# A written-out order of every queue in place of a greedy scheduler: clustered attention and a gated long convolution on one core

## The chip, the core and the metric

The kernel runs on one core of one Trainium2 chip. Five engines work from queues of their own: PE (TensorE, matrix products into PSUM), DVE (VectorE), ACT (ScalarE), POOL (GpSimd) and SP (SyncE, which here only issues transfers). The metric is device microseconds of one execution. Several executions are timed, and their median is the time of the kernel; one more is profiled.

## The reference

Two parts, cut to what matters. The first is attention in which a query sees only the keys of its own cluster (batch 4, 8 heads, 768 positions, 64 values a head, 16 centroids a head):

```python
q_assign = np.argmax(np.einsum('bhsd,hcd->bhsc', q_n, c_n), axis=-1)
k_assign = np.argmax(np.einsum('bhsd,hcd->bhsc', k_n, c_n), axis=-1)
mask = q_assign[:, :, :, None] == k_assign[:, :, None, :]
scores = scale * np.matmul(q, k.transpose(0, 1, 3, 2))
scores = np.where(mask, scores, -1000000000.0)
scores = scores - np.max(scores, axis=-1, keepdims=True)
attn = np.exp(scores)
attn = attn / (np.sum(attn, axis=-1, keepdims=True) + 1e-09)
return np.matmul(attn, v).astype(np.float32)
```

The second takes its output, as (4, 768, 512), through a gated convolution over the whole sequence:

```python
proj = x @ w_proj
x1, x2, x3 = (proj[..., :D], proj[..., D:2 * D], proj[..., 2 * D:])
X2 = np.fft.rfft(x2, n=S, axis=1)
H = np.fft.rfft(filter_fft, n=S, axis=0)[None, :, :]
x2_conv = np.fft.irfft(X2 * H, n=S, axis=1)
y = x1 * x2_conv * x3
return (y @ w_out).astype(np.float32)
```

## The kernel before

**Work.** `build` describes the whole computation as a list of 1917 operations, made in the order of the mathematics. An operation (`Plan.op`) holds a function that emits its instructions, the engines that may run it with an estimated duration on each, what it reads and writes, and, where it writes PSUM, a `Bank` that it allocates and later operations free. PSUM has eight banks; banks 4 and 5 together hold the attention output (`pair`) for most of the run.

**Stages.** Attention runs in 8 groups `n` (a batch element and half of its heads), each of 2 pairs of heads `pr`, so 16 blocks. Before a group, `routing(n)` transposes its queries and keys on PE (L564, L575), evicts them into `qkP` (L265 on ACT or L267 on DVE), casts them into the bf16 tiles `aug` (the same lines; ACT, DVE or POOL), multiplies with the centroids (L484, L595), finds the nearest centroid on DVE (L616 to L633) and puts the one-hot rows into `aug` by transfers (L469), so that one product gives the masked scores. A block (`attention`) has 6 steps of 128 keys. A step is 3 score operations on PE (`sc`, through the helper `product`, L73 and L75), 3 exponentials on ACT into `p` (L678, L681) and one value product of 8 matmuls into `pair` (L692). The row sums are built on DVE by adding the `p` tiles into `acc` (L713); the first sum of a block is split into three parts that DVE or POOL can run (`part`, L709). Then ACT copies the output to `osb` (L716), the denominators come from a matmul (`den`, L726) or, in the middle groups, from transfers that add rows (L746), their reciprocal (L759) is spread over the partitions by transfers (L760, L763), and DVE writes the normalised output `xT` (L792).

After every second group `hyena(b)` runs the convolution of one batch element, between the products of the next attention blocks: projections (L824), spectra (L75, L458), products with the filter's spectrum on DVE (L848), their sums `y` on DVE or POOL (L852), gates `x3` (L885, L888), inverse transforms (L75), evictions `od` and `sd` (L911, L913), folds on DVE or POOL (`fold`, L923), the gated result `y2` (L926) and the output product, evicted into `ob` (L946) and stored (L953). `tables` makes the transform tables and the filter's spectrum `hm` (L441 to L445) at the start, `weights` loads `w_proj` in four pieces (`wpj`, L1020) and `w_out` (L1023) from POOL's queue. `load_qk` (L302) and `load_v` (L308) load queries, keys and values from SP's queue, the first ones also from ACT's.

**Who sets the order.** Every instruction order is fixed when the program is built. `Plan.place` simulates the five engines with the estimated durations: each time it takes the engine that can start earliest, and for it, among the operations that could start within `wait` of the earliest one, the one with the smallest due time. The due time of an operation is written at its `op(...)` call and shifted by its entry in the table `NUDGE` (some 1900 numbers). Further terms are costs: a change of PE's array mode (`shape`), two value products in a row (`bonus`), an operation on DVE that another engine could run (`BUSY`). `ONLY` pins an operation to one engine. `banks_for` picks the PSUM banks: those that come free first, at most `HELD` banks each for the scores and for the rest. The result is one list sorted by planned start; the program is emitted in that order, so the list is each engine's queue. An engine never overtakes: an operation that waits holds all behind it on the same engine.

**PE's array mode.** `array` gives each PE operation a mode: 128 columns, 64 or 32. A score or projection takes the mode of the operation ahead of it, if that was 64 or 128; in 64 `product` emits it as two halves.

**POOL and DVE.** An operation with `lock` on POOL waits for the last `lock` operation that stands before it on DVE (the last lines of the kernel's function, at the end of the file).

Of the kernel before, what the change touches and what calls it, by code (L numbers as in the profile page):

```python
# [35 lines left out]
LEAD = 2.99901  # L36
FIRST = 2
BUSY = 8.09741
HELD = 4
# [38 lines left out]
class Plan:  # L78

    def __init__(self):
        self.ops, self.writers, self.reads = [], {}, {}

    def op(self, eng, fn, due, r=(), w=(), alloc=None, free=(), lock=False, byts=0, after=(), kind=None, lat=0.0):
        o = Op()
        o.eng = eng if isinstance(eng, dict) else {eng[0]: eng[1]}
        o.fn, o.due, o.alloc, o.free, o.lock, o.byts, o.kind = fn, due, alloc, free, lock, byts, kind
        o.seq = len(self.ops)
        o.due += NUDGE.get(o.seq, 0.0)  # L90
        o.outs, o.end, o.start, o.on = [], None, None, None
# [15 lines left out]
        for d in deps:  # L107
            d.outs.append(o)
        for h in free:
            h.readers += 1  # L110
        self.ops.append(o)
        return o

    def place(self, free0, banks_for, switch=0.1, wait=0.1, rate=215e3, bonus=10.84378, margin=0.02195, shape=1.63806):
        free = dict(free0)
        bank_free = [0.0] * 8
        ready = {e: [] for e in free}
        pend = 0
        st = SimpleNamespace(pool=0.0, dve=0.0, bw={}, last=None, kind=None, score=0, o=0, tail=0,
                             held=dict(score=0, fill=0, o=0))  # L120
# [3 lines left out]
        def enqueue(o):  # L124
# [4 lines left out]
            for e in o.eng:  # L129
                ready[e].append(o)  # L130
# [1068 lines left out]
```

## Time and profile before

| | before |
|---|---|
| time, median of 3 runs | 386.62 us (385.18 to 389.62) |
| span of the profiled execution | 383.4 us |
| PE busy | 366.2 us, 96% |
| DVE busy | 335.8 us, 88% |
| ACT busy | 258.7 us, 67% |
| POOL busy | 115.3 us, 30% |
| TensorE clock granted, mean | 0.997 |
| moved by DMA | 47.19 MB |

The span runs from the first to the last instruction of the profiled execution; its own run time outside that span is not given, so the time of the runs, 3.2 us longer at the median, stands beside it. Busy times are unions over an engine's instructions. In the rows of groups the parts are: line, engine, operation, tile written and tiles read, shapes, count, busy us, mean ns of one, and the idle time of the engine just before them with what ended it. Line numbers are those of the kernel before. A matmul's end is modelled in the profile, and matmuls in different columns of the array overlap, so eight value matmuls of 490 ns mean take 1.30 us together.

### The profile page before, as it was taken

The numbers are of one execution on the slowest core, as the hardware profiler recorded it, in microseconds if no ns is written. First come the engines' busy times: TensorE is split into PE (matmuls) and PEld (weight loads), VectorE is DVE, ScalarE is ACT, GpSimd is POOL, SyncE is SP. The second block draws the span as 40 slices with busy tenths as digits, with TensorE's granted clock in tenths as the row PEclk, the third lists the DMA queues.
The fourth block names the chain that finished last, engine by engine and source line by source line (L and its number), as shares of the span: only waits on it lengthen the run. The fifth ranks groups of instructions, "written<-read, shape, count | busy, mean of one in ns | idle before, by whom it ended". The sixth has DMA issues, their size and how long they took to land.

```text
span 383.4 us, 8667 instructions
## 1 busy us (share of the span) xinstructions
PE 366.2 (96%) x3337; PEld 223.0 (58%) x3343; DVE 335.8 (88%) x497; ACT 258.7 (67%) x483; POOL 115.3 (30%) x155
## 2 busy tenths in 40 slices
PE   3999997999999999999999999999999899999995
PEld 2555454445455564655465665667578566557883
DVE  8778797888899689988999997998998899999982
ACT  5998878787885986588784656877762458712142
POOL 8522302011014454322342443222330452212500
PEclk9999999999999999999999999999999999999998
DMA  9909967642688678466986888854666641200124
GB/s 174 237 21 208 192 151 153 149 96 78 138 164 163 111 145 143 97 114 105 194 132 163 124 166 212 131 77 77 105 97 162 146 68 9 78 11 2 55 113 164
DMA packets 93861, 47.19 MB, mean 123 GB/s; under 512 B 82088, under 2 KB 87676, under 8 KB 93820
## 3 DMA queue, kind: packets, MB, share of 16 engines
q1 hardware_dynamic: 87836, 36.84, 43.3%
q0 software_dynamic: 2704, 8.98, 16.3%
q10 hardware_dynamic: 3280, 0.82, 1.2%
q8 instruction: 26, 0.43, 0.5%
q14 instruction: 15, 0.12, 0.1%
HBM read 31.59 MB, written 7.40 MB: 102 GB/s over the span
## 4 chain that ended last, share of the span: by engine, by line
PE 73%; DVE 17%; ACT 4%; issue 3%; POOL 1%; DVEq 0%; POOLq 0%; ACTq 0%
PE bank L75 30%; PE pair L692 24%; DVE acc L713 8%; PE bank L824 6%; PE bank L564 3%; PE bank L73 2%; PE bank L595 2%; PE bank L458 2%; DVE hm L445 1%; ACT p L681 1%; PE bank L726 1%; PE bank L608 1%; PE bank L575 1%; ACT qkP L265 1%; DVE mx L616 1%
## 5 line engine op out<-in xcount | busy, mean ns | idle before, releaser
L692 PE MATMUL pair<-p,vraw 128*64 128x385 f32 x768 | 143.1, 490 | 0.3 <-ACT osb L716 0.2
L681 ACT ACTIVATE p<-bank 128x512 f32<-128x512 f32 x192 | 110.1, 609 | 26.3 <-PE bank L75 20.1
L713 DVE TENSOR_TENSOR acc<-p,acc 128x1536 f32<-128x1536 f32 x64 | 112.9, 1763 | 10.6 <-POOL acc L709 4.4
L692 PEld LDWEIGHTS pair<-p,vraw 128*64 128x64 f32 x768 | 56.1, 136 | 46.2 <-issue 39.0
L75 PE MATMUL bank<-aug,aug 128*64 128x256 bf16 (+3 forms) x652 | 70.2, 326 | 1.4 <-DVE tm L267 1.3
L678 ACT ACTIVATE p<-bank 128x512 f32<-128x512 f32 x96 | 58.0, 608 | 12.3 <-PE bank L75 12.1
L75 PEld LDWEIGHTS <-aug 80*64 80x64 bf16 (+1 forms) x652 | 40.0, 109 | 33.5 <-issue 23.0
L746 POOL DMA_DIRECT2D acc<-acc x30 | 24.2, 807 | 65.6 <-DVE acc L713 26.0
L75 PE MATMUL bank<-xT,wpj 128*64 128x384 bf16 x448 | 41.5, 326 | 0.0
L709 POOL TENSOR_TENSOR acc<-p,p 128x512 f32<-128x512 f32 x22 | 28.1, 1282 | 44.0 <-DVE acc L709 21.1
L267 POOL CAST aug<-qkP 64x768 bf16<-64x768 f32 x22 | 18.0, 821 | 68.9 <-DVE acc L713 25.7
L75 PEld LDWEIGHTS <-y 128*64 128x64 bf16 x512 | 29.8, 110 | 9.8 <-issue 4.8
L265 ACT COPY qkP<-bank 128x512 f32<-128x512 f32 (+1 forms) x47 | 23.7, 542 | 17.4 <-PE bank L75 9.4
L75 PEld LDWEIGHTS <-wpj 128*64 128x64 bf16 x448 | 28.0, 110 | 11.9 <-issue 3.8
L848 DVE TENSOR_TENSOR tm<-bank,hm 128x512 f32<-128x512 f32 x44 | 28.5, 683 | 4.8 <-POOL y L852 1.6
L852 POOL TENSOR_TENSOR y<-tm 128x512 bf16<-128x512 f32 x17 | 21.5, 1273 | 23.3 <-DVE acc L713 9.6
L265 ACT CAST aug<-qkP 64x768 bf16<-64x768 f32 x31 | 25.7, 829 | 1.7 <-DVE qkP L267 0.5
L75 PE MATMUL bank<-wout,y 128*64 128x512 bf16 x192 | 23.1, 379 | 0.0
L824 PE MATMUL bank<-wpj,xT 128*64 128x512 bf16 x192 | 22.6, 380 | 0.0
L709 DVE TENSOR_TENSOR acc<-p,p 128x512 f32<-128x512 f32 x26 | 17.7, 700 | 2.5 <-ACT p L681 1.8
L716 ACT COPY osb<-pair 128x770 f32<-128x770 f32 x16 | 12.9, 804 | 9.8 <-PE pair L692 9.6
L923 POOL TENSOR_TENSOR yy<-sd 128x384 f32<-128x384 f32 x9 | 9.0, 1003 | 33.4 <-DVE acc L713 15.1
(154 smaller groups left out, 456.9 us busy)
## 6 DMA issues: line engine op xcount, KB each, us to landing
vraw<-in_v_dram SPq DMA_DIRECT2D x16, 384.0 KB, 4.5
qkraw<-in_q_dram SPq DMA_DIRECT2D x30, 192.0 KB, 4.7
qkraw<-in_k_dram SPq DMA_DIRECT2D x30, 192.0 KB, 5.2
rb<-dr SPq DMA_DIRECT2D x30, 192.0 KB, 3.5
out_dram<-ob SPq DMA_DIRECT2D x11, 512.0 KB, 3.1
acc<-acc POOLq DMA_DIRECT2D x10, 384.0 KB, 5.6
acc<-acc POOLq DMA_DIRECT2D x10, 192.0 KB, 4.0
y<-in_moe_filter_fft_dram SPq DMA_DIRECT2D x4, 384.0 KB, 5.2
```

The costliest lines, as they stand in the source:

```text
L75: T.nc.tensor.matmul(out[64 * i:64 * i + 64], lhsT[:, 64 * i:64 * i + 64], rhs, start=start, stop=stop)
L265: T.nc.scalar.copy(out, in_)
L267: (T.nc.vector if e == "DVE" else T.nc.gpsimd).tensor_copy(out, in_)
L678: T.nc.scalar.activation(o, ap(h).rearrange("p (a b) -> p a b", a=2), Act.Exp, scale=0.125)
L681: T.nc.scalar.activation(flat(s)[:, lo:lo + 512], ap(h), Act.Exp, scale=0.125)
L692: T.nc.tensor.matmul(o[64 * hp:64 * hp + 64, ch, :385], T.vraw[vs][:, hp, sk * D:(sk + 1) * D], T.p[slots[sk]][:, hp, 384 * ch:384 * ch + ...
L709: alu(e).tensor_tensor(o, x, y, op=Alu.add)
L713: T.nc.vector.tensor_tensor(T.acc[os], T.p[slots[sk]][:, :, :S], T.acc[os], op=Alu.add)
L746: op(("POOL", .8), lambda e, rows=rows: T.nc.gpsimd.dma_start(flat_()[:rows], flat_()[rows:2 * rows], accum_op=Alu.add), te, r=[], w=AK, b ...
L824: T.nc.tensor.matmul(ap(h)[64 * i:64 * i + 64], T.xT[xs][:, kt, c:c + 64], T.wpj[:, kt, DM:2 * DM], start=kt == 0, stop=kt == ND - 1)
L848: op(("DVE", .68), lambda e, i=i, cs=cs, r=r, h=h: T.nc.vector.tensor_tensor(T.tm[r][:, cs], ap(h), hmrow(i, (0, 2, 2, 3)[2 * r + cs]), op ...
L852: op({"POOL": 1.5, "DVE": .68}, lambda e, i=i, r=r: alu(e).tensor_tensor(T.y[:, i, r], T.tm[r][:, 0], T.tm[r][:, 1], op=Alu.add if r else ...
```

## The change

`Plan.place` and `banks_for` go, with the due-time shifts `NUDGE`, the pins `ONLY` and the scheduler's constants. In their place stands a string `ORDER` with one word for each operation: a letter for the engine, the number of the operation in the list of `build`, and after a colon the PSUM banks where it allocates some. `Plan.follow` reads the words, sets engine and banks, and returns the operations in the order of the words; PE's array mode follows from that order by the same `array` as before. The operations themselves, their functions, what they read and write, and the emission are untouched. The due times in `build` stay in the file and are no longer read.

```diff
 ROWS = 16
-LEAD = 2.99901
 FIRST = 2
-BUSY = 8.09741
-HELD = 4
 EARLY = 8.73655
-NUDGE = {0:-2.65714,1:-0.164318,2:15.6428,3:104.959,
...
-ONLY = {23:"SP",24:"SP",25:"SP",26:"ACT",27:"ACT",29:"SP",30:"ACT",53:"ACT",
...
+ENGINE = {"P": "PE", "A": "ACT", "V": "DVE", "G": "POOL", "S": "SP"}
 THIRDS = [[(0, 0, 512)], [(0, 512, 768), (1, 0, 256)], [(1, 256, 768)]]
-HOLD = {"score": "score", "o": "o"}
-AFTER = {"PE": .16}
-OVERLAP = {"ACT": .09, "DVE": .08}
...
-        o.due += NUDGE.get(o.seq, 0.0)
...
-    def place(self, free0, banks_for, switch=0.1, wait=0.1, rate=215e3, bonus=10.84378, margin=0.02195, shape=1.63806):
...
-        return sorted(self.ops, key=lambda o: (o.start, o.seq))
...
-def banks_for(bank, free, st, o):
...
+    def follow(self, order):
+
+        placed, last = [], None
+        for word in order.split():
+            name, _, banks = word.partition(":")
+            o = self.ops[int(name[1:])]
+            o.on = ENGINE[name[0]]
+            if banks:
+                o.alloc.ids = tuple(map(int, banks))
+            if o.on == "PE":
+                last = array(o, last)
+                o.whole = last == 128
+            placed.append(o)
+        assert len({o.seq for o in placed}) == len(placed) == len(self.ops)
+        return placed
+
+
+ORDER = """
+G8 A15 S24 A23 G13 S26 A25 G1 S27 G10 V4 S28 V16 V17 G0 V18 V43 A19 S29 G7 V6 V31 S108 V37 G2 V20 P54:0 G5 P52:1 G9
...
+P349:1 P355:3 V323 G353 P357:2 A350 P359:6 S324 P363:7
...
+V1897 P1899 A1900 S1901
+"""
...
-    order = P.place({"PE": .3, "ACT": .8, "DVE": .8, "POOL": .8, "SP": .8}, banks_for)
+    order = P.follow(ORDER)
     return P, order
```

Counted over both built programs, 129 operations change their engine (the rest of the difference is place and bank). By line, the number on each engine before and after:

| operation | ACT | DVE | POOL |
|---|---|---|---|
| casts into `aug` (operation at L581) | 31, 23 | 11, 12 | 22, 29 |
| first sums `part` (L701) | | 26, 28 | 22, 20 |
| products `y` (L852) | | 7, 16 | 17, 8 |
| folds (L917) | | 23, 29 | 9, 3 |
| gated result `y2` (L926) | | 15, 14 | 1, 2 |
| evictions into `qkP` (L567, L577) | 40, 42 | 12, 10 | |
| evictions `x3`, `od` (L885, L911) | 37, 41 | 11, 7 | |
| tables `inv`, scaling (L407, L411, L439) | 11, 10 | 4, 5 | |

More of the change, by code (lines that the diff above doesn't have):

```diff
@@ L223, in banks_for @@
-def banks_for(bank, free, st, o):
-    def whole(lo, hi):
-        return max(free[lo:hi])
-    if bank.cls == "o":
-        t = whole(4, 6)
-        return ((4, 5), t) if t < 1e8 else None
-    allowed, first = [0, 1, 2, 3, 6, 7], []
-    if st.score and st.score < st.scores:
-        if st.held["score" if bank.cls == "score" else "fill"] + bank.n > HELD:
-            return None
-    if st.o == 0:
-        allowed += [4, 5] if bank.cls == "head" else []
-    elif st.o == st.otiles:
-        if st.tail:
-            allowed += [4, 5]
-        elif whole(4, 6) < 1e8:
-            first += [4, 5]
-    t = lambda i: whole(4, 6) if i in first else free[i]
-    ids = sorted((i for i in allowed + first if free[i] < 1e8), key=lambda i: (t(i), i))[:bank.n]
-    return (tuple(ids), max(map(t, ids))) if len(ids) == bank.n else None
+    def follow(self, order):
[12 more added lines that the diff above has]
+        return placed
@@ new lines @@
+G669 P767:1 P747 S712 V519 S711 V520 S710 V756 P521:0 S709 P769:7 P755 A770 A768 V522 P848:637 V524 V523 V764 P526:1
+A850 S886 P763 A849 A766 A851 V772 P529:0 P786:2 P788:3 P790:6 A787 P793:7 V527 P771 A791 G774 A789 V525 S670 V530
+S887 G855 P537:2 A773 V528 P795:6 S713 P797:3 G853 A794 P792:45 V531 A796 V533 A798 P803:1 V854 S671 P805:7 P807:0
+V532 P534:6 A806 S715 A808 S847 P811:3 G801 P813:7 V536 P799 S885 A814 V535 A804 S888 V538 G775 A812 P856:076 V539
+A852 V800 P815:1 P542:3 A858 V859 A857 V540 P544:2 A816 V541 P819:0 A543 P821:6 P546:7 V802 V672 P823:1 P827:3 A547
@@ new lines @@
+P809 A824 V673 V545 S674 A820 G776 V810 A822 P829:7 P831:1 P893:2 P895:0 P817 A894 V818 A862 S675 A828 P864:62 S676
+A832 V826 A830 S777 P548:3 A865 S889 A866 P825 A896 V834 P867:17 S778 V549 G860 P897:2 S892 P900:6 V870 P902:0 P904:3
+V868 G863 P833 A903 S891 V869 A905 V677 G836 A898 P550:03 A901 V871 A835 P557:2 G907 V551 P910:6 V552 P899:45 A911
+V553 V872 P912:1 V873 P914:7 P918:6 P920:0 P922:3 P906 A921 V874 V875 A919 V908 S876 A913 P926:0 V554 A558 P928:6
+P559:1 V555 A923 G837 V556 A915 P561:2 A927 P563:3 V562 G909 A929 P930:7 V779 P916 V780 V560 S781 V564 P934:0 S954
@@ new lines @@
+P572:2 V917 S877 P936:6 G838 P565:13 A573 S878 A937 P924 A566 G861 S782 A931 V568 S880 V925 P938:2 P932 S783 A939 A935
+S879 P1131:672 S890 V933 S882 S839 P1069:0 P940 A1133 V567 S1170 A1134 V941 A1070 S884 P574:1 A1132 A942 P576:3 V569
+G943 S840 P1071:0 V570 P1073:2 S1168 P578:6 A1072 V577 G1138 A1074 V575 P1076:7 S881 P1078:0 P1080:3 V1135 S883
+P1086:2 P1075:45 V784 A1087 A1081 V579 A1077 P1088:1 P1090:2 V571 A1079 P1094:3 P1096:6 P587:7 A1089 V1084 A1091
+P1098:0 V1085 P1102:1 A1097 P1082 V588 G1083 A1103 V841 P1104:2 V842 P1092 S843 A1105 G944 V1093 A1095 P1106:6
@@ new lines @@
+P1139:712 A1107 G1136 A1099 S845 P1110:3 V1101 P580:60 A1142 S1169 A1140 P1100 A581 S1171 G945 A1141 V583 S844 A1137
+V582 P589:1 S1172 A1111 P1112:2 P1114:7 V590 P1147:06 A1113 V585 A1143 V1109 P1176:3 P1178:1 P1108 A1177 V584 A1115
+S946 V1117 P1180:2 S1175 P1183:3 P591:7 A1181 P1185:2 P1116 A592 V1149 G1119 A1148 V586 A1179 S947 A1184 P1187:7
+P1150:06 V846 A1118 P593:1 A1186 V1151 G1144 A1188 P1193:3 V1153 P1195:2 P1182:45 V1152 G1146 A1196 V1154 V594 P1197:7
+V1192 P1201:2 P1203:0 V1191 P1205:6 A1202 P1189 G1120 A1206 V1155 A1198 V1156 A1204 P1209:1 P1211:2 P595:67 A1194
@@ new lines @@
+A1318 P1009:0 V1129 A1317 P1345:3 A615 P1319:12 A1010 G992 S616 A1315 P1347:7 P1277 V1320 A1284 V1322 A1348 G1314
+V1323 A1313 P1285 V1321 V1286 P1349:0 P1011:6 S1406 A1350 P1352:7 A1346 V1324 G1288 P1354:1 P1356:2 V1012 A1353
+P1362:0 P1013:3 A1287 V1359 P1002:67 A1014 V1325 P1351:45 A1003 A1357 V1326 V1327 A1355 P1015:3 V1005 G1361 S1328
+A1363 V1004 P1364:2 P1366:1 V1231 P1370:0 P1372:6 A1367 P1374:7 V1232 P1358 V1360 A1371 S1233 A1365 V1007 G1289 A1373
+V1016 P1378:1 P1017:02 V1006 A1375 V1369 P1380:3 P1382:6 P1386:7 A1381 P1368 S1234 A1018 A1379 S1332 V1019 A1383 S1235
@@ new lines @@
+P1024:3 V1020 A1387 V1377 S1330 P1026:1 G1290 S1329 P1388:6 P1583:027 A1389 S1334 V1385 S1336 S1331 P1390:6 P1376
+A1585 A1842 V1008 A1391 P1384 V1022 S1291 A1025 V1393 P1521:6 P1392 A1522 A1586 V1584 P1523:3 G1590 P1525:6 S1292
+P1528:0 A1524 P1028:2 A1526 V1236 P1530:7 A1529 P1030:3 A1394 V1029 G1588 P1532:6 P1538:0 P1540:2 A1531 P1527:45 V1021
+G1395 A1541 V1027 A1533 G1536 V1031 A1539 P1542:7 P1546:2 P1548:1 A1589 P1550:6 P1554:3 P1534 V1535 A1543 V1293 A1555
+V1294 P1556:0 V1023 P1558:7 S1295 P1039:3 A1557 S1582 A1551 V1537 P1544 A1559 S1335 V1545 A1040 G1396 S1333 A1547
@@ new lines @@
+P1495:7 V1494 P1791:4 V1740 A1496 P1499:56 V1485 A1792 P1793:2 P1497:7 V1794 V1486 P1795:4 V1487 V1483 P1796:2 V1489
+V1500 P1799:0 V1797 P1802:1 V1488 V1798 P1806:3 V1502 G1490 P1807 V1501 P1800 P1809:4 A1808 V1498 P1810 V1801 P1803
+P1815:2 V1805 G1504 P1813:5 V1804 V1811 G1503 P1843:6 V1814 P1845:3 V1816 G1505 P1847:7 V1817 P1818:0 A1848 V1812
+A1844 P1821:1 V1820 P1829:5 V1819 P1837:2 V1823 P1826:7 V1822 P1506:4 V1825 V1828 P1849:6 A1507 V1831 P1511:0 V1824
+P1856:1 V1827 G1833 P1508:4 A1857 V1830 A1512 P1834:7 V1846 A1509 G1832 P1516:1 V1836 S1510 V1850 P1858:5 V1839
```

167 lines of the change are left out of this document (63 added, 104 removed).

## The prediction

> **What bounds the kernel now.** I read the page's busy line first, then who waited for whom on PE, then the busy time by stage, then the groups by shape, and last the chain.
>
> ```profile
> span 383.4 us, 8667 instructions
> PE 366.2 (96%) x3337; PEld 223.0 (58%) x3343; DVE 335.8 (88%) x497; ACT 258.7 (67%) x483; POOL 115.3 (30%) x155
> ```
>
> PE is busy for 366.2 of 383.4 us. The order decides when PE's work is done, hardly how much there is, so the most that an order can give back is PE's 17.2 us of idle time. The waits of PE say where these are:
>
> ```profile
> PE bank L575 <- DMA qkraw<-in_q_dram: 6.3, 1, 6.3
> PE bank L75 <- DVE tm L267: 1.3, 1, 1.3
> PE bank L73 <- ACT p L681: 1.0, 2, 0.8
> PE bank L726 <- DVE dn L759: 0.8, 1, 0.8
> PE bank L484 <- ACT qkP L265: 0.5, 1, 0.5
> PE bank L73 <- ACT aug L265: 0.5, 1, 0.5
> PE bank L73 <- DVE qkP L267: 0.5, 1, 0.5
> PE bank L333 <- DVE sd L330: 0.4, 1, 0.4
> PE bank L726 <- DVE acc L713: 0.4, 1, 0.4
> PE pair L692 <- ACT osb L716: 0.2, 1, 0.2
> ```
>
> Columns: who waited, for whom, us in total, times, longest. 6.3 us is the first load, which every order needs. The nine other waits sum to 5.6 us: these an order can close. PE's last matmul ends at 379.0 us by the timeline, so 4.4 us is the tail of eviction and store. The remaining 0.9 us is gaps too short for the list. The stages, each ending where a block's output leaves PSUM:
>
> ```profile
> 0.00:22.00 22.00, 14.32 (x112) 9.78 (x113) 17.40 (x46) 17.26 (x33) 13.39 (x52) 1.00 0.91 181
> 57.90:77.20 19.30, 17.23 (x140) 8.38 (x139) 16.20 (x21) 15.88 (x29) 2.93 (x4) 1.00 0.69 155
> 129.00:150.60 21.60, 21.55 (x168) 11.84 (x167) 17.02 (x23) 17.58 (x32) 9.99 (x10) 1.00 0.85 147
> 150.60:165.60 15.00, 15.00 (x154) 8.63 (x150) 14.03 (x27) 8.55 (x16) 6.40 (x7) 1.00 0.52 94
> 165.60:187.70 22.10, 21.90 (x185) 12.49 (x186) 19.29 (x24) 19.62 (x37) 7.00 (x8) 1.00 0.81 147
> 187.70:204.60 16.90, 16.67 (x145) 9.57 (x144) 15.77 (x27) 12.73 (x24) 5.23 (x6) 1.00 0.86 148
> ```
>
> Columns: stretch, length, busy PE, PEld, DVE, ACT, POOL, clock, DMA share, GB/s. PE loses time before 22 us, between 57.9 and 77.2, and once near 297 us (the 1.3 us wait); from 129 to 204.6 it hardly idles at all. The clock is granted in full.
>
> **The change, part by part.** No operation is added or taken away: both programs hold the same 1917 planned operations. Three things differ: positions, PSUM banks, and the engine of some 130 operations. Counting the two built orders, and pricing with these rows:
>
> ```profile
> L852 POOL TENSOR_TENSOR y<-tm 128x512 bf16<-128x512 f32 x17 | 21.5, 1273 | 23.3 <-DVE acc L713 9.6 <-DVE tm L848 6.6 <-DVE aug L267 3.4
> L852 DVE TENSOR_TENSOR y<-tm 128x512 bf16<-128x512 f32 x7 | 5.1, 727 | 0.1
> L267 POOL CAST aug<-qkP 64x768 bf16<-64x768 f32 x22 | 18.0, 821 | 68.9 <-DVE acc L713 25.7 <-DVE aug L267 22.5 <-ACT osb L716 10.1
> ```
>
> - DVE takes 9 products `y` (0.727), 6 folds (0.576), 2 first sums `part` (0.700), 1 cast of `aug` (0.563), 2 copies of `inv` (0.25) and 1 short `qkP` copy (0.556); it gives up 3 `qkP` copies (0.664), 2 `x3` and 2 `od` copies (0.55 each), 1 scaling (0.751) and 1 `y2` product (0.949). Net +7.1 us: 335.8 becomes about 343.
> - POOL loses the 9 products (1.273), the 6 folds (1.003) and 2 sums (1.282), and gains 7 casts (0.821) and one `y2` (1.821): -12.5 us.
> - ACT loses 8 casts (0.829) and 2 `inv` copies (0.316), gains 7 copies and a scaling for 4.4 us and loses one of 0.478: -3.3 us.
> - PE does the same products. It changes its array mode 70 times where it was 73. In the chain a value product (8 matmuls) takes 1.45 us after a change and 1.30 us without one, so 0.15 x 3 = -0.45 us; bounds 0 and -0.45; I take all of it, since PE is the bound.
>
> DVE's 7.1 us costs nothing as long as DVE's own idle time (383.4 - 335.8 = 47.6 us) covers it where it falls; without that cover it is +7.1.
>
> What is on PE's path, wait by wait:
>
> - First load. Its two halves were the first two issues of SP, 1.38 us for both from 0.74, so the second was out at 2.12 us. Now one half is SP's first and the other ACT's second issue, which was out at 1.77 us before: -0.35 at most, 0 if landing and not issue decides. I take -0.3.
> - Start (0.4 + 0.5 + 0.5 = 1.4 us of waits for `sd`, `qkP` and `aug`). ACT, busy 17.26 of 22 us, hands 2 casts and 3 copies to others before the first block's exponentials end, and the centroid norm moves up in DVE's queue, ahead of four of the angle steps. Two of the three waits are for DVE's `sd` and for an ACT copy, the third for a cast whose chain keeps its steps; I take a third as closed: -0.5; bounds -1.4 (all closed) and +0.8 (one cast of 0.82 us that now waits on POOL).
> - Around 58 to 62 us (`qkP` 0.5, `p` 0.8, `dn` 0.8: 2.1 us). DVE is late here: the last sum of the second block ends at 62.0 us, and the denominator matmul (L726) stands behind it, with the same five PE operations ahead of it in both orders. Before that DVE waited 2.0 us for PE and 0.8 us for ACT at the rows `hm` (L445). The written order puts a sum (1.76 us) ahead of three operations of that kind which it stood behind and gives a fourth to ACT, so two thirds of these waits have work to fill them: -1.4; bounds -2.1 and +1.0, since DVE has some 1 us more work by then.
> - Around 91 to 94 us (0.4 + 0.2 us). The denominator matmul is queued two score operations later, and both sets of transposes (1.46 us each) come before the last value products, so DVE's last sum has that much more cover: -0.5; bounds -0.6 and 0.
> - At 297 us (1.3 us): PE waited for a bank that DVE evicted (`tm`), DVE being behind a sum. The written order gives one more of these evictions to ACT (0.59 us, ACT was idle 2.1 us beside it) and puts a projection (L75, 0.65 us) among the seven long products. -1.2; bounds -1.3 and 0.
> - Tail: the last eviction moves from DVE (0.69) to ACT (0.59): -0.1.
> - New waits that PE has not now: between 129 and 204.6 us DVE takes 5 products, 4 folds, 3 sums and 2 copies more and gives 2 copies up: 3.64 + 2.30 + 2.10 + 1.37 - 1.22 = +8.2 us, where it idles 4.58 + 0.97 + 2.81 + 1.13 = 9.5 us. It fits by 1.3 us. I take +0.25 between 0 and +8.2: PE's waits show none for DVE in these stages, and the products that move take 0.73 us instead of 1.27.
>
> [...]
>
> Sum: -0.3 - 0.5 - 1.4 - 0.5 - 1.2 - 0.1 - 0.45 + 0.25 = -4.2 us. The profiled span of 383.4 becomes 379.2. The runs' median is 386.62, 3.2 above the span of the profiled execution; I carry the difference over unchanged: 386.62 - 4.2 = 382.4 us.
>
> **The rivals.**
>
> - The gaps move. Each closed wait reappears elsewhere, since PE, DVE and their banks leave little room (PE 96%, DVE 88%). Only the head, the tail and the array changes stay: -0.85, so 385.8. For it: five of the nine waits are under 0.6 us, no longer than one eviction. Against: the two largest have a plain cause, DVE late at one place, and the order changes just that.
> - Slower: DVE becomes the bound from 129 us on. The 9.5 us that DVE idles there are waits for PE or POOL; if none of them can be filled, all 8.2 us land on PE, and DVE's 1 us more in the first two blocks also keeps the 1.4 us near 60 us. -4.45 + 1.4 + 8.2 = +5.15: 391.8. It decides once more than 1.3 us of that idle time is unusable. For it: DVE ends up at 98% there. Against: 17 POOL operations run in about half the time on DVE, and DVE waited 7.4 us for such operations (`acc` 4.4, `tm` 1.6, `y` 1.4).
> - The weights bunch. Three of the four `wpj` loads are now issued together, in the second block, where they stood some 12 us apart. In the profile a load lands 5.2 us after its issue. DMA is 77% busy at 170 GB/s in that stage (40.2 to 57.9 us). If the two extra loads hold the next group's `qkraw` and the mask rows back by one landing, PE waits about 5.2 us once: -4.2 + 5.2 = +1.0, 387.6. Against: that group's loads are still queued some 12 us of PE work or more ahead of their use. [...]
>
> That the order is the old one written out is excluded: the engine counts differ.
>
> **How the numbers follow.** A measurement of this kernel can tell about 1% (3.9 us) from no change; the three runs shown span 385.2 to 389.6. Forecast 0.52 (0.43 of it faster by over 1%, 0.09 within); gaps move 0.22, all within; DVE bound 0.17 (0.15 slower, 0.02 within); weights 0.09 (0.05 within, 0.04 slower). Faster 0.43, same 0.38, slower 0.19. If all nine waits close, the time is -0.35 - 5.6 - 0.45 - 0.1 = -6.5, so 380.1: the range starts just below, at 379.5. At the top it reaches into the DVE case, to 390.0. The forecast's own range is 379.5 to 385.0.
>
> **What would show it.** Right: PE's busy time within 1 us of 366; its waits other than the first load at 2 to 3 us, none over 0.8; the denominator matmul without a wait; DVE near 343 us, POOL near 103. Wrong: a PE wait for DVE between 129 and 205 us; DVE idle time there still above 4 us with PE idle beside it; a PE wait for `qkraw` or `aug` rows between 60 and 80 us.

## The result and the profile after

| | before | after |
|---|---|---|
| median, the result | 385.30 us (383.39 to 389.62, 10 runs) | 382.65 us (381.64 to 383.95, 10 runs) |
| median, beside experiments 6 to 8 | 388.62 us (386.31 to 391.46, 17 runs) | 382.50 us (381.27 to 383.77, 6 runs) |
| span of the profiled execution | 383.4 us | 382.2 us; a second one 380.1 us |

The ratio is 0.9916 with a 95% interval of 0.9896 to 0.9936 in the result (2.5 to 4.0 us less) and 0.9835 (0.9801 to 0.9869) beside experiments 6 to 8. Both intervals lie below 1; the first saving is under 1%, the second over it. The new kernel's median moved by 0.2 us between its two sets of runs, while the old one's was 385.3, 386.1, 388.0 and 388.6 in four, so what before measures in a set weighs on every ratio. Ratios are of fast runs: six of the 23 runs of before beside experiments 5, 9 and 10, and one of the second-and-third-block kernel in 10, count as slow and stand in the medians and ranges alone. The profiled execution of after (383.95 us, of which 1.75 lie outside the span) is the slowest of its ten, so a second profile of the same kernel stands beside it below.

Line numbers of the kernel after are those of before less 22 in `build` (L575 is now L553) and less 8 in `product` (L73 and L75 are L65 and L67); in experiments 4, 5 and 6 the string `ORDER` is a line shorter, so lines behind it are one less again. The page of after:

```profile
span 382.2 us, 8637 instructions
PE 365.9 (96%) x3343; PEld 213.9 (56%) x3346; DVE 341.5 (89%) x509; ACT 252.7 (66%) x480; POOL 102.7 (27%) x146
```

PE does the same work, DVE 5.7 us more, POOL 12.6 and ACT 6.0 less. Who waited for whom on PE (us in total, times, longest):

```profile
PE bank L553 <- DMA qkraw<-in_q_dram: 5.5, 2, 5.3
PE bank L462 <- DVE cbd L317: 1.6, 1, 1.6
PE bank L472 <- ACT sim L243: 1.4, 1, 1.4
PE bank L65 <- ACT qkP L243: 0.7, 1, 0.7
PE bank L67 <- ACT tm L419: 0.7, 1, 0.7
PE bank L67 <- DVE hm L423: 0.7, 1, 0.7
PE bank L802 <- DVE ob L245: 0.3, 1, 0.3
PE bank L378 <- ACT fw L345: 0.3, 1, 0.3
PE bank L553 <- DMA qkraw<-in_k_dram: 0.2, 1, 0.2
```

The waits near 60 us for `p` and `dn`, at the denominator matmul near 93 us and for the evicted `tm` at 297 us are gone. Before had none of those that stand in their place. Two fall in the first 17 us: 1.6 us for the centroid copies `cbd` and 1.4 us for a similarity eviction `sim`. Two more are in every profile whose order is the written one there: 0.7 us near 51 us for `tm`, here ACT's scaled table (L419), and 0.7 us near 60 us for DVE's rows `hm` (L423). Waits other than the first load sum to 5.9 us, no less than before's 5.6. The same stretches as shown of before (length, busy PE, PEld, DVE, ACT, POOL, clock, DMA share, GB/s):

```profile
0.00:22.00 22.00, 12.96 (x76) 7.90 (x77) 16.26 (x42) 13.32 (x25) 12.36 (x51) 0.92 0.95 180
57.90:77.20 19.30, 18.63 (x154) 9.20 (x151) 15.22 (x21) 16.40 (x30) 5.43 (x5) 1.00 0.63 141
129.00:150.60 21.60, 21.55 (x174) 11.26 (x173) 20.73 (x30) 16.25 (x33) 7.52 (x9) 1.00 0.67 111
150.60:165.60 15.00, 14.94 (x152) 9.00 (x147) 14.51 (x26) 8.71 (x18) 4.97 (x6) 1.00 0.68 134
165.60:187.70 22.10, 21.42 (x198) 12.39 (x200) 20.48 (x28) 16.67 (x33) 5.42 (x7) 1.00 0.79 132
187.70:204.60 16.90, 16.85 (x137) 9.71 (x135) 16.39 (x28) 11.12 (x23) 4.51 (x6) 1.00 0.81 126
```

The start got worse (by 22 us PE has been busy for 12.96 us instead of 14.32), and its clock reads 0.92. From 57.9 to 77.2 us PE is busy 1.4 us longer. In the last four stretches DVE is busy 72.1 of 75.6 us where it was 66.1, and PE idles for 0.8 us in all. The groups that moved:

```profile
L830 DVE TENSOR_TENSOR y<-tm 128x512 bf16<-128x512 f32 x16 | 10.8, 686 | 0.2
L830 POOL TENSOR_TENSOR y<-tm 128x512 bf16<-128x512 f32 x8 | 10.1, 1271 | 12.8 <-DVE y L830 6.0 <-DVE xT L770 3.8 <-DVE tm L826 3.0
L245 POOL CAST aug<-qkP 64x768 bf16<-64x768 f32 x29 | 23.7, 823 | 62.2 <-DVE acc L691 28.8 <-ACT qkP L243 14.3 <-DVE dn L737 13.1
```

**Where the time went.** Cut at the ends of value products, PE's idle time in a stage is its length less its busy time. Before, for the stages from the start to the last value product of the first block, on to that of the second, on to the first one of the third, and from the last of the fourteenth to the first of the fifteenth:

```profile
0.00:39.98 39.98, 32.24 (x263) 19.53 (x265) 31.80 (x69) 33.74 (x67) 17.50 (x57) 1.00 0.82 161
39.98:57.32 17.34, 17.10 (x136) 8.36 (x132) 14.38 (x14) 12.57 (x24) 3.80 (x4) 1.00 0.77 169
57.32:65.79 8.47, 6.40 (x54) 3.57 (x55) 7.77 (x10) 7.41 (x14) 2.11 (x3) 1.00 0.72 151
291.16:306.81 15.65, 14.34 (x135) 10.69 (x132) 12.76 (x20) 6.10 (x11) 5.66 (x6) 1.00 0.60 130
```

The same stages in the second profile of after:

```profile
0.00:41.87 41.87, 33.12 (x264) 19.12 (x266) 32.82 (x71) 31.69 (x62) 16.92 (x55) 0.96 0.77 149
41.87:59.57 17.70, 16.99 (x137) 8.52 (x133) 15.67 (x17) 15.22 (x28) 3.28 (x5) 1.00 0.91 190
59.57:67.82 8.25, 7.58 (x72) 3.87 (x73) 5.71 (x8) 7.31 (x14) 4.62 (x4) 1.00 0.47 106
290.04:301.94 11.90, 11.90 (x116) 6.75 (x114) 9.84 (x15) 8.30 (x16) 3.63 (x4) 1.00 0.65 133
```

The idle time is 7.74, 0.24, 2.07 and 1.31 us before, 8.75, 0.71, 0.67 and 0 after. Lengths are not compared beyond the first stage, since the order puts other work between the same products. All stages, in the same way (us, against before):

| part | forecast | first profile of after | second |
|---|---|---|---|
| first block: PE idle | -0.8, with the next row | +1.63 | +1.01 |
| first block: PE busy | | +0.77 | +0.88 |
| second block: idle | | +0.47 | +0.47 |
| to the third block's first value product (58 to 62 us): idle | -1.4 | -1.40 | -1.40 |
| around 91 to 94 us: idle | -0.5 | -0.65 | -0.65 |
| 97 us to the tenth block's end: idle | +0.25 | +0.35 | -0.54 |
| on to the fourteenth block's end: idle | | +0.19 | -0.21 |
| around 297 us, and after it: idle | -1.2 | -1.27 | -1.27 |
| PE busy after the first block | -0.45 | -1.14 | -1.41 |
| tail | -0.1 | -0.17 | -0.17 |
| sum | -4.2 | -1.22 | -3.29 |

So the later waits close much as forecast (3.3 us in the three rows near 60, 93 and 297 us), and the first block, by its end 2.40 and 1.89 us later than before, takes back more than half of that. The experiments went into that start.

### The profile page after: what moved, and what is told of

It is laid out like the page before. It is cut to its first block, busy times and chain, and to the rows that moved or that the text cites. A ratio compares the mean times of both kernels' runs of the same rounds, so it can differ in the third digit from the quotient of the medians.

```text
span 382.2 us, 8637 instructions
## 1 busy us (share of the span) xinstructions
PE 365.9 (96%) x3343; PEld 213.9 (56%) x3346; DVE 341.5 (89%) x509; ACT 252.7 (66%) x480; POOL 102.7 (27%) x146
## 4 chain that ended last, share of the span: by engine, by line
PE 86%; DVE 5%; ACT 4%; DMA 2%; issue 1%; POOL 0%; SPq 0%; DVEq 0%; ACTq 0%; POOLq 0%
PE bank L67 35%; PE pair L670 30%; PE bank L802 5%; PE bank L542 4%; PE bank L65 3%; PE bank L573 3%; PE bank L436 2%; DMA rb<-dr 2%; PE bank L586 1%; PE bank L704 1%; ACT tm L419 1%; ACT qkP L243 1%; PE bank L462 1%; DMA dr<-dn 1%; DVE ob L335 1%
## 5 line engine op out<-in xcount | busy, mean ns | idle before, releaser
L691 DVE TENSOR_TENSOR acc<-p,acc 128x1536 f32<-128x1536 f32 x64 | 113.3, 1771 | 7.9 <-POOL acc L687 2.8
L670 PEld LDWEIGHTS pair<-p,vraw 128*64 128x64 f32 x768 | 53.7, 136 | 48.7 <-issue 42.7
L67 PE MATMUL bank<-aug,aug 80*64 80x256 bf16 (+3 forms) x706 | 77.5, 326 | 1.4 <-ACT tm L419 0.7
L67 PEld LDWEIGHTS <-aug 80*64 80x64 bf16 (+1 forms) x706 | 41.7, 109 | 39.0 <-issue 27.0
L67 PE MATMUL bank<-xT,wpj 128*64 128x384 bf16 x448 | 44.3, 326 | 0.0
L245 POOL CAST aug<-qkP 64x768 bf16<-64x768 f32 x29 | 23.7, 823 | 62.2 <-DVE acc L691 28.8
L243 ACT COPY qkP<-bank 128x512 f32<-128x512 f32 (+1 forms) x50 | 26.2, 551 | 21.5 <-PE bank L67 8.4
L67 PEld LDWEIGHTS <-wpj 128*64 128x64 bf16 x448 | 28.8, 109 | 11.8 <-issue 4.4
L67 PEld LDWEIGHTS <-y 128*64 128x64 bf16 x464 | 24.5, 110 | 9.9 <-issue 3.0
L67 PE MATMUL bank<-wout,y 128*64 128x512 bf16 x176 | 22.1, 379 | 0.0
L243 ACT CAST aug<-qkP 64x768 bf16<-64x768 f32 x23 | 19.0, 828 | 1.0 <-PE bank L65 0.7
L243 ACT COPY x<-bank 128x384 f32<-128x384 f32 x20 | 9.7, 492 | 14.2 <-PE bank L67 10.7
L542 PEld LDWEIGHTS bank<-ident,qkraw 128*128 128x128 f32 x144 | 15.5, 140 | 5.5 <-issue 3.3
L542 PE MATMUL bank<-ident,qkraw 128*128 128x128 f32 x144 | 18.1, 277 | 0.0
```

The costliest lines, as they stand in the source:

```text
L67: T.nc.tensor.matmul(out[64 * i:64 * i + 64], lhsT[:, 64 * i:64 * i + 64], rhs, start=start, stop=stop)
L243: T.nc.scalar.copy(out, in_)
L245: (T.nc.vector if e == "DVE" else T.nc.gpsimd).tensor_copy(out, in_)
L542: T.nc.tensor.transpose(bank(h.ids[i // 4])[:, ts(i % 4, 128)], raw(ss[i // NT], i % NT), T.ident)
L670: T.nc.tensor.matmul(o[64 * hp:64 * hp + 64, ch, :385], T.vraw[vs][:, hp, sk * D:(sk + 1) * D], T.p[slots[sk]][:, hp, 384 * ch:384 * ch + ...
L691: T.nc.vector.tensor_tensor(T.acc[os], T.p[slots[sk]][:, :, :S], T.acc[os], op=Alu.add)
```

## The experiments

An edit is given in words of `ORDER`. A "set" is the kernels that ran beside the same runs of before, to which the ratios refer. Experiments 1 to 4 are the first set (before 386.05 us), 5, 9 and 10 the second (387.95), 6, 7 and 8 the third (388.62). The written order itself ran in the third set alone; where another set's kernel is compared with it, the medians of different sets stand side by side.

**1. The old start, then the written order** (109 of the 129 changes of engine are kept):

```diff
-G8 A15 S24 A23 G13 S26 A25 G1 ...   (written order, to the first value product, 165)
+G0 A15 S23 A26 S24 G1 A27 V6 S25 ...   (order of before, to the same product)
 ...   (the rest: written order)
```

> The queues up to the first value product (number 165, the first 230-odd words) are those of the kernel before, all that follows stands in the written order. Theory: the written order loses about 2.5 us in its start (first score at 24.8 us in its profile instead of 21.7) and gains 3.8 to 5 us later, so this runs 2 to 2.5 us below the written order, near 380.3 us, with the first score near 21.7 us. Rival: the late start belongs to the one profiled execution (its loads landed late), and the gain of the other runs is spread over the whole; then this is within 0.5 us of the written order, near 382.6.

Measured: 381.36 us (380.49 to 381.97), ratio 0.9871 (0.9839 to 0.9902), so 1.1 to 1.3 us below the written order. The sign is the theory's, the size about half. Its profile ends the first block at 40.16 us, 1.7 and 2.2 us ahead of the written order; but PE then waits 1.1 us at one score product near 164 us, for mask rows (`aug<-ohT` by transfer). At the same product the written order's first profile waits 0.7 us for `qkP`, and its second and experiment 7's not at all, so this wait comes and goes with the execution. Why the median gains only half of what the theory said is not shown.

**2. The written start, then the old order:**

```diff
 G8 A15 S24 A23 G13 S26 A25 G1 ...   (written order, to value product 165)
-...   (written order)
+...   (order of before)
```

> The reverse: the written order up to the first value product, then the queues of the kernel before. Theory: the start costs its 2.5 us and nothing gives them back, so 2 to 2.6 us above the kernel before, near 387.7. Rival (the start is no slower in general): within 0.5 us of the kernel before.

Measured: 389.5 us (387.64 to 393.22), ratio 1.0077 (1.0037 to 1.0116): the kernel with the written start is slower than the old one by 1.4 to 4.5 us. That is the sign expected and 1.8 us above the time expected. The first block ends at 41.89 us, 1.9 later than before. Not all of that is the start's: the first score product comes at 22.92 us, 1.2 later than before, and just behind the joint of the two orders, at 31 us, PE waits 1.2 us for `p`, which neither kernel does there. Another 1.6 us are lost later, in a stretch whose queue is the same as before's; there the clock reads 0.50 for 3.40 us, taken up below.

**3 and 4. What is late in the start.** The two timelines (start, length in us) show it. Before:

```profile
5.87 1.28 ACT L365 ACT_TABLE_LOAD   x1
9.09 0.21 DVE L338 COPY cbd<-bank 64x64 f32<-64x64 f32 x1
11.11 2.42 PE L484 MATMUL bank<-qkP,cbd 128*32 128x384 f32 x8
12.92 0.47 ACT L265 COPY sim<-bank 64x384 f32<-64x384 f32 x1
14.44 0.58 PE L494 MATMUL bank<-ident,sim 64*128 64x64 f32 x6
```

After:

```profile
9.81 1.28 ACT L345 ACT_TABLE_LOAD   x1 [1.16 <-DVE ob L340]
11.11 0.20 DVE L316 COPY cbd<-bank 64x64 f32<-64x64 f32 x1
11.70 1.48 PE L462 MATMUL bank<-qkP,cbd 128*32 128x384 f32 x8 [1.60 <-DVE cbd L317]
14.53 0.46 ACT L243 COPY sim<-bank 64x384 f32<-64x384 f32 x1
16.39 0.90 PE L472 MATMUL bank<-ident,sim 64*128 64x64 f32 x6 [1.42 <-ACT sim L243]
```

DVE copies the centroids 2.0 us later, because their word (V22) stands behind the angle steps in DVE's queue, though the norm itself (V20) did move up. ACT loads the sine's table at 9.81 us, between two evictions of `qkP`, where before it lay in idle time at 5.87 us. And a similarity eviction stands behind the sines. Experiment 3 moves the copies alone:

```diff
-... P21:2 V3 V44 ... A35 S110 V22 P82:6 ...
+... P21:2 V3 V22 V44 ... A35 S110 P82:6 ...
```

> The written order with one word moved: the copies of the centroids into cbd (V22) stand right behind V3 on DVE instead of behind eight operations of the angles and two evictions. Theory: PE's wait of 1.6 us for cbd shrinks, but the second wait of the start, for an eviction on ACT behind the table load, remains, so 0.3 to 1.0 us below the written order. Rival: cbd is covered by the late eviction on ACT anyway (both end at 11.5 to 12.1 us): no change, within 0.3 us.

Measured: 382.59 us (382.05 to 383.62), ratio 0.9909 (0.9875 to 0.9943), the same as the written order. The rival holds: the 1.6 us wait goes, the 1.4 us wait for `sim` stays, and the first score product comes at 24.33 us, between the written order's 24.29 and 24.78. Experiment 4 also puts the sine that loads the table (A50) ahead of an eviction, with what it reads (V3) ahead of the norm:

```diff
-... V20 P54:0 G5 P52:1 G9 A55 ... V3 V22 ... P64:0 A50 V83 ...
+... V3 V20 P54:0 G5 P52:1 G9 A50 A55 ... V22 ... P64:0 V83 ...
```

> As the one before, and the two small sines (A50) stand ahead of the first eviction on ACT, with their input (V3) ahead of the norm on DVE, so the table load for the sine (1.28 us) falls into ACT's idle time before 6.2 us instead of between two evictions at 9.8 us. Theory: the two together are what the start loses: 1.5 to 2.5 us below the written order, near 380.6. Rival: the start is bound elsewhere (loads of the second keys landing after 8.8 us): less than 0.7 us.

Measured: 381.68 us (380.46 to 384.57), ratio 0.9891 (0.9851 to 0.9932); first score product at 23.74 us. It is half of the gain expected, with the widest scatter of the mended starts, so the gain is not clear of it; the 1.4 us wait for `sim` is still there. The scatter goes with the clock: the three runs with a mean granted clock of 1.000 took 380.46 to 381.11 us, the three with 0.994 to 0.996 took 382.25 to 384.57.

**5. All the heads of queue that wait, moved back:** both similarity evictions behind their products (A67, A65), the table transposes behind the similarity transposes (P124), a copy that waits for PE behind the one-hot chain (V131).

```diff
-... P66:7 V40 ... P64:0 V83 A42 S114 A67 ... A63 P124 P88 A65 ... P68:5 ...
+... P66:7 A67 V40 ... P64:0 A65 V83 A42 S114 ... A63 P88 ... P68:5 P124 ...
```

> On top of the two moves of the run before (cbd earlier, small sines first): on ACT the two evictions of the similarities (A67, A65) stand right behind the products that they evict, ahead of five sines; on PE the transposes of the table (P124) stand behind the transposes of the similarities (P68) instead of ahead of them; on DVE one copy of a table (V131) stands behind the last step of the one-hot chain (V73). Theory (a handful of queue heads that wait for something late make the whole loss of the start): first score at 22 us or earlier, time 0.5 to 1.5 us below the run with the two moves, near 380.5 us, level with the old start in front of the written order. Rival (the start is bound by the landings of keys and queries, PE's transposes wait for them at 19 us): the first score stays at 23.5 us or later, the time within 0.4 us of the run with two moves.

Measured: 381.62 us (380.99 to 381.90), ratio 0.9821 (0.9772 to 0.9870), first score product at 23.13 us, between theory and rival, and a time within 0.1 us of experiment 4, as the rival said. The wait for `sim` falls from 1.4 to 0.3 us, but its list of PE's waits has a new one:

```profile
PE bank L310 <- DVE sd L307: 1.2, 1, 1.2
```

It is the norm. The mending puts one more step ahead of it (V3 ahead of V20, 0.2 us), but experiment 4 has the same words there and no such wait: its norm's last step starts at 6.51 us, this one's at 7.12. In this execution two DVE steps ahead of the norm (L962, L296) took 0.83 and 0.76 us, in experiment 4's 0.17 and 0.32, so most of this wait is not the order's.

**6. The norm first**, on top of 5:

```diff
-... V6 V31 S108 V37 G2 V3 V20 P54:0 ...
+... V6 V20 V31 S108 V37 G2 V3 P54:0 ...
```

> The mended start (centroid copies, sine, similarity evictions, one-hot chain) with the centroid norm on DVE ahead of the first four angle steps. In the mended start PE waits 1.2 us for the scaled centroids and its first score product comes at 23.1 us. Theory (each of the heads of queue that wait costs PE its time until the next one takes over): that wait goes, first score near 22.3, 381.0, that is 0.6 below the mended start. Rival (the angle steps pushed back delay the sines and with them the table products and the similarity evictions on ACT): first score 23 or later, 381.6 or more.

Measured: 381.72 us (379.97 to 383.34), ratio 0.9814 (0.9777 to 0.9850), first score product at 23.69 us. The rival holds. The timeline of ACT has the table load, in experiment 5 and then here, at:

```profile
6.20 1.28 ACT L353 ACT_TABLE_LOAD   x1 [1.21 <-DVE kp L955]
```

```profile
8.40 1.28 ACT L353 ACT_TABLE_LOAD   x1 [3.41 <-DVE kp L955]
```

The wait for `sd` is gone; ACT now gets its operand `kp` 2.2 us later, and PE waits for the tables `fw` instead (1.5 us in two waits, where it had 0.6). Start waits can be handed round: DVE and ACT share one chain of small steps, and here the word moved up pushed another down.

**7. The first load, alone.** The old start with the written order behind it (experiment 1), its first loads issued half by SP, half by ACT, and the first two transposes changed round to follow the landing:

```diff
-G0 A15 S23 A26 S24 G1 A27 V6 S25 A28 ... P52:0 A50 G8 P54:1 ...
+G0 A15 S24 A23 S26 A25 S27 S28 G1 V6 ... P54:0 A50 G8 P52:1 ...
```

> The start of the old order, then the written order, with one thing of the written start: the first queries and keys are issued half by SP and half by ACT, and their transposes follow the landing. Theory (the first load was under-sized: it moves the first matmul from 6.3 to about 5.3 us, and PE has queued work right behind it): first score product near 21.0 us where the old start has 21.9, and 380.4, 1.0 below the 381.4 of the old start with its own loads. Rival (the start is bound by the chain centroid norm, similarity, one-hot, mask, which the queries' landing does not lead): first matmul earlier, first score product still at 21.7 to 21.9, time 381.4 within 0.4.

Measured: 380.95 us (380.04 to 381.35), ratio 0.9790 (0.9759 to 0.9822). Against the written order in the same set (382.50) it is 1.55 us faster, and the best of all kernels here. First score product at 21.44 us against 21.93: half of what the theory wanted. The first matmul came 1.0 us earlier (5.43 us against 6.42), and then PE waited for the next thing, by the list of waits:

```profile
PE bank L311 <- DVE sd L308: 1.3, 1, 1.3
```

The old start's norm is ready at 8.2 us in either case, and the late load had hidden most of that wait (0.3 us in experiment 1). The same edit on the kernel before:

> The kernel before with its first loads split in the same way and nothing else. Theory: first matmul near 5.3 us, first score product near 20.8, about 0.9 us below the kernel before at the median. Rival: first score product at 21.7 within 0.2 and no difference. The old middle scatters by several us, so the profile's first 40 us decide rather than the median.

Measured: 386.24 us (384.49 to 389.61), ratio 0.9955 (0.9920 to 0.9989). First matmul 5.42, first score product 21.31 against 21.74 us, PE's end 0.69 us earlier; the same 1.3 us wait for `sd`. Both answers lie between theory and rival: PE starts 0.9 to 1.0 us earlier, and about half of that is left at the first score product. That an earlier norm would bring the rest is argued; this start with its norm moved up was not run.

**8. The written order again,** beside 6 and 7:

> The written order itself, unchanged, beside the three others on one chip. Every theory: 382.65 within 0.5 us, first score product near 24.8 us of the span, and again the waits for the centroid copies (1.6 us) and for the similarity eviction (1.4 us) in the start; if these two are an accident of one execution they are missing here.

Measured: 382.50 us; first score product 24.29 us, with the waits for `cbd` (1.0 us) and `sim` (1.4 us) once more. The later waits of the first profile, for `qkP` (0.7 us, near 166 us) and `ob` (0.3 us), are absent: those came with the execution, the ones in the start did not.

**9. DVE and POOL.** Nine products `y` and seven folds back from DVE to POOL, at the places that the written order has for them:

```diff
-V (16 words of products y and folds)
+G (the same 16 words)
```

> The written order with the engine letter of 16 words put back: the nine products y and the seven folds that went from POOL to DVE run on POOL again, at the same places of the list. Theory (the moved work is a real part of the gain, since POOL takes 1.27 and 1.00 us where DVE takes 0.73 and 0.58 and a POOL operation waits for DVE's sum before it): new waits of PE for banks and inverse transforms in the stages from 110 us on, 1.5 to 5 us above the written order, 384 to 388 us. Rival (DVE has slack, and PE does not see where these run): within 0.7 us of the written order; and the rival of the prediction that DVE is overloaded there would have it faster.

Measured: 383.05 us (382.35 to 384.28), ratio 0.9864 (0.9818 to 0.9910). That is 0.4 to 0.6 us above the written order's medians from other sets, within the scatter, and not the 1.5 to 5 us of the theory: which of the two engines runs these 16 operations hardly matters to PE.

**10. Regions of the order by themselves.** The written order only between value products 285 and 369 (second and third block), and only behind 1667 (the last two blocks):

```diff
 ...   (order of before, to value product 285)
-...   (order of before, to 369)
+...   (written order, to 369)
 ...   (order of before)
```

> The queues of the kernel before, except that between two value products (numbers 285 and 369, some 45 to 72 us) they stand in the written order. Theory: the waits of PE at 58 to 62 us (2.1 us with the hidden part, 2.5) shrink to some 0.6, so 1.5 to 2 us below the kernel before, near 384.2. Rival (the gain there is only lateness pushed on): within 0.5 us of the kernel before.

Measured: 385.76 us (384.40 to 390.22), ratio 0.9988 (0.9950 to 1.0026): inconclusive, and not the 1.5 to 2 us of the theory. The idle 2 us at 58 to 62 us are gone in its profile, but its list of PE's waits has one that neither kernel has, where the two orders meet again:

```profile
PE bank L67 <- DVE oh L596: 1.1, 1, 1.1
```

> The queues of the kernel before up to a value product at 291 us (number 1667), then the written order to the end. Theory: the one wait at 297 us (1.3 us) goes and the eviction at the end is 0.1 us shorter, so 1.2 to 1.8 us below the kernel before, near 384.5. Rival (it reappears further on in the last stage): within 0.5 us of the kernel before.

Measured: 386.04 us (384.10 to 389.51), ratio 0.9955 (0.9915 to 0.9996). The wait at 297 us is gone, with 0.3 us for `ob` in its place: from the end of the fourteenth block to 307 us its profile has 0.26 us of PE idle, where before had 1.31. The gain (0.2 to 3.3 us) takes in the forecast 1.2, though only just clear of none.

**The clock, seen in these traces.** In the profile of after, the stretch ahead of the similarity transposes and the one behind it:

```profile
12.99:16.40 3.41, 1.69 (x15) 1.02 (x13) 1.97 (x4) 3.36 (x9) 1.72 (x10) 1.00 1.30 215
16.40:19.82 3.42, 3.42 (x14) 1.25 (x14) 2.35 (x5) 2.44 (x4) 2.58 (x5) 0.50 0.90 205
```

PE was busy for 1.69 of 3.41 us, and then its clock stood at 0.50 for 3.42 us (called a spell here); the eight similarity matmuls in it took 847 ns at the median where the eight ahead of it took 486. The second profile of after reads 0.50 at 17.30 to 20.71 us, and the profiles of experiments 3 and 4, which kept the 1.4 us wait, read it from 18 to 20.5 and from 17 to 19 us. Before and experiments 1, 5, 6 and 7 have none there. Neither have experiments 2 and 9, whose queues are the written order's up to there: in their profiles the matmuls were slow from the start until about 16 us (six transposes at 14.07 and 14.70 us took 1.49 us, where the same six took 0.85 at 13.48 us in after), and no 1.4 us wait came. With one queue up to the first value product, then, the first block ended at 41.2 to 42.4 us, and the slow stretches fell in different places; what part of that spread is theirs was not separated. The 0.8 and 0.9 us by which PE's busy time in the first block grew in the two profiles fit a slower PE behind the 1.4 us wait.

The waits alone do not make up the lateness of the start. PE's idle time in the first block, the first load included, is 7.74 us before and 7.96, 7.88, 7.99, 7.77 and 7.57 us in experiments 2, 3, 4, 5 and 9, yet their first blocks end at 41.89, 41.83, 41.34, 40.73 and 41.15 us against 39.98. There nearly all of the lateness is busy time: 32.96 to 33.95 us, against 32.24. (PE starts 0.8 to 1.2 us earlier in these five, so the waits behind the first load are longer by about as much.) Only the two profiles of the written order (9.37 and 8.75 us) and experiment 6's (8.54) idle clearly longer. How much of the added busy time is the clock was not separated.

Experiment 2 has a spell at the gap near 62 us that the old order leaves:

```profile
60.77:64.18 3.41, 1.40 (x9) 0.46 (x12) 3.41 (x5) 3.03 (x6) 2.02 (x3) 1.00 0.57 153
64.18:67.58 3.40, 3.40 (x22) 1.40 (x24) 2.34 (x5) 1.78 (x4) 0.00 (x0) 0.50 0.84 159
```

Here the queue is before's own and the gap is the same: PE idles 2.08 us in that stage (2.07 before), and the stage takes 10.08 us instead of 8.47, all of it busy time. In before's profile PE was busy 1.80 us of the 3.41 from 59.30, and the clock read 1.00 in the 3.41 us behind. So one and the same gap cost 2.1 us in one execution and 3.7 in another, and in the second the clock read 0.50 for 3.40 us.

The spells took 3.42, 3.41 and 3.40 us (after, its second profile, experiment 2). In the stretch of that length ahead of each PE was busy for 1.69, 1.69 and 1.40 us, and for 1.98 in experiment 4 (from 12.97 to 16.39 us). Busy time by itself does not decide: the 3.41 us from 9.58 us in after have 1.81 us of it and no spell behind them. What sets a spell off is not shown.

Spells may also be why the old kernel scatters. Of the 48 runs of before that enter the ratios of the experiments, the 8 with a mean granted clock of 0.991 or less have a median of 389.4 us and the 13 with 0.998 or more 385.3 us (correlation of time with lost clock 0.64; 0.62, 0.71 and 0.42 in the three sets by themselves). In the 16 runs of after it is 0.14. One spell of 3.41 us at half the clock lowers the mean by 0.0044 (1.705 of 383.4 us). Low clock behind PE's last matmul counts in that mean and holds up no matmul (before's profile reads 0.55 from 381.0 us to its end, with PE busy for none of it), so the relation is loose. No run forced or forbade a spell, so for the single runs this is argued and not shown.

## Why the prediction was right, and where it was not

The time was forecast at 382.4 us, and 382.65 was measured. That it came so close is luck, since two errors offset each other: the saving was 2.65 us by the medians and not 4.2, and before's median beside it was 385.3 and not 386.62. Of the 3.2 us that the prediction carried over from span to median, 1.8 lie outside the span in the runs listed; the rest was before's scatter. Of the forecast's chance of 0.52, 0.43 stood on a saving of over 1%; the result's ratio is 0.84% below 1, the later one 1.65%.

**First load (-0.3): under-sized, and cashed only in part.** Over all profiles PE starts at 6.41 us on average with the old issue (four profiles) and at 5.33 with the split one (ten), 1.1 us earlier. The prediction took the issue's own saving of 0.35 for the upper bound; PE's start gained three times that. The order of the loads changed too: before, ACT issued a load of keys at 1.16 us, between the two halves of the first queries, and now both halves go first. Which of the two made the difference was not separated. Experiment 7 shows half of it lost to the norm.

**Start (-0.5): the step that failed.** It argued from engine counts and from the norm's new place that a third of 1.4 us would close. Counts say nothing of who stands at the head of a queue. Measured, with the first load in it: +2.40 and +1.89 us at the end of the first block. The bound given (+0.8, for one cast on POOL) was of another thing. The waits came from the centroid copies and the similarity eviction, which are behind angle steps and sines in their queues, and the clock spell (0.50 for 3.4 us) came on top. Experiments 1 and 2 show the sign from both sides, the second with a wait at its joint; 3 to 6 show which words PE waited for. What each is worth they leave open: the copies moved alone brought nothing, and the mended starts end within 0.1 us of one another at 381.6 to 381.7 us.

**58 to 62 us (-1.4), 91 to 94 us (-0.5), 297 us (-1.2), tail (-0.1): right**, at -1.40, -0.65, -1.3 and -0.17. The reason given, an operation late on DVE and more cover ahead of it, agrees with the waits that went. Near 60 us the size is part luck: all three named waits went (2.1 us), not two thirds of them, and a new one of 0.7 us for `hm` took the place of the rest. In experiment 10 the last two blocks by themselves agree with the term at 297 us; the second and third block by themselves close the gap near 60 us, and what that is worth could not be priced.

**Array modes (-0.45):** PE's busy time fell by 1.1 to 1.4 us behind the first block, and experiments 1 and 7, with the same order there, have it too (332.85 and 332.88 us against before's 333.99). The fall sits in the value products, whose busy time there is 134.28 us before and 132.00 and 132.02 after. By the prediction's price the modes explain 0.45 of it; the rest is not separated, and the two profiles of after, one and the same kernel, list 3343 and 3346 matmuls.

**New waits (+0.25):** +0.35 in one profile and -0.54 in the other between 97 us and the tenth block's end. The second block, of which nothing was said, added 0.47: it is the 0.7 us wait for the scaled table `tm` near 51 us.

**The rivals.** DVE as the bound falls: it is busy 72.1 of 75.6 us there, and PE idles 0.8 us in one profile and nothing in the other. The bunched weights fall: DMA is busy for 0.91 of the second block's time, and no PE wait in it is for a load. "The gaps move" is half true: they did close where forecast, and their sum came back (5.9 for 5.6 us), 3.5 us of it in the start, 1.4 near 51 and 60 us, and 1.0 later in the first profile alone. The stated sign for it, waits of 2 to 3 us and none over 0.8, is the one that failed; the others (PE 365.9, DVE 341.5, POOL 102.7 us, no wait at the denominator matmul) came as said. The prices by engine were rough, DVE +5.7 for +7.1 and ACT -6.0 for -3.3 us, but neither is on PE's path. Beside the seven added POOL casts, DVE's 64 sums took 1771 ns each instead of 1763.

**"The clock is granted in full"** was read off the column and holds for before's profile from 13 us to PE's last matmul (128x128 transposes of 273 ns at the median), not ahead of it (421 ns; last section).

## What to carry to other kernels

Read a written order by the heads of the queues: for every engine, which word waits, for whom, and which ready words stand behind it; counts per engine do not show that. Splice two good orders at a point where both have done the same work, since each has its own strong region: the old start under the written rest, with split loads, beat both. Then look at the joint, where two of the spliced kernels had a new wait of 1.1 or 1.2 us. And count a wait of PE for more than its length where PE's work is thin around it: in experiment 2 a gap of 2.08 us cost 3.7, with the clock at 0.50 for the next 3.40 us.

## What the runs showed of the hardware that was not expected

- A spell of half clock lasted 3.4 us and followed 3.4 us in which PE was busy for 1.4, 1.7 or 2.0 us (experiments 2, after and 4). Two other stretches of 3.41 us, with 1.80 us (before, from 59.30) and 1.81 us (after, from 9.58), had none behind them, so busy time alone does not tell. The stage with the spell in experiment 2 took 10.08 us, where before's took 8.47.
- The clock column does not show the slow start. It reads 1.00 from 0 us, yet PE's first 128x128 transposes take 421 ns at the median (before and after) and later ones 273. By these durations PE runs slowly from its first matmul to 9.4 us in after, about 12.5 us in before and 16 us in experiment 2; of the same eight similarity matmuls at 11 to 12 us, the start timelines above have 1.48 us in after and 2.42 in before.
- With the first load issued by two engines and both halves of the queries ahead of the keys, PE starts at 5.33 us on average instead of 6.41, 1.1 us earlier, for an issue that is out 0.35 us earlier.
